# A second level of pairwise comparison in a top-k attention kernel, and another way to split its weights

## The chip, the cores and the metric

The kernel runs on one core of a Trainium2 chip. The metric is device time in microseconds (us). The engines are TensorE (PE, matmuls and transposes), VectorE (DVE), ScalarE (ACT), GpSimd (POOL) and SyncE (SP, which here issues all DMAs). Each works through its own queue in order.

## The reference

Attention with 4 batches, 8 heads, 576 positions and 64 dimensions, in which each query keeps its 32 largest scores; the result, 2304 rows of 512, goes through a gated feed-forward layer.

```python
scores = scale * np.matmul(q, k.transpose(0, 1, 3, 2))
kth = np.partition(scores, -top_k, axis=-1)[..., -top_k:-top_k + 1]
scores = np.where(scores >= kth, scores, -1000000000.0)
scores = scores - np.max(scores, axis=-1, keepdims=True)
attn = np.exp(scores)
attn = attn / (np.sum(attn, axis=-1, keepdims=True) + 1e-09)
x = np.matmul(attn, v)            # then heads side by side, 512 wide
xn = x / np.sqrt(np.mean(x * x, axis=-1, keepdims=True) + 1e-06) * rms_g
g = xn @ w_gate
out = (g / (1.0 + np.exp(-g)) * (xn @ w_val)) @ w_out
```

The three weight matrices (512 x 1536, 512 x 1536, 1536 x 512) arrive as float64.

## The kernel before

**Attends.** An attend is two heads times 128 query rows; there are 72. PE forms the scores (12 matmuls of 288 columns, fp32 split into a high and a low fp32r part), ACT copies them from PSUM into one of 5 slots `sp`, and DVE finds the 32nd largest of each row (`topk`, L492). For each of the two heads `e`, L511 and L512 take minimum and maximum of the two halves of the row: 32 values among 576 can only be among the 288 maxima and the few largest minima, so L513 appends the 8 largest minima to the maxima, and four rounds of L516 (8 largest) and L518 (replace them by a very small number) run over 296 elements. POOL turns the result into a threshold (L546) and stores a difference `gap`, from which the end of the kernel sees whether 8 minima were enough; if not, an exact second program runs (it does not here). ACT and POOL mask and exponentiate (L550 to L552), PE transposes (L575) and multiplies by V.

**Feed-forward.** When all heads of 256 query rows (a unit) are done, `feed_forward` (L627) normalizes and runs blocks: 24 matmuls for gate and value, ACT's tanh (L721), DVE's two products (L727, L728), ACT's and POOL's split into high and low part, and 6 matmuls with a slice of `w_out` in a slot `wo`. The first unit is done as two tiles of 128 rows with 6 blocks each (there a block covers two slices), eight more have 12 blocks: 108 in all.

**Weights.** In 36 pieces of 128x512 (`weight_piece`, L337), 512 KB each as float64. A piece lands in a raw tile (`xvt`, and `tg` or `kraw`, in turn), DVE joins the bits of its two words (L357 into a PSUM bank, L358 into one of three temporary tiles), ACT takes a Sign (L359) that POOL adds for rounding (L360), ACT casts the high part (L365) and POOL subtracts it for the low part (L368). The 12 slices of `w_out` also go to a scratch in DRAM (`wosc`), from which each later unit loads them again (L702) into 2 slots `wo`. All pieces are converted while the first unit is worked on.

**Order.** The program adds operations with an engine, a duration and a priority from the table `PR`; a planner (`place`, L99, with `emit`, L211) places them in a simulated time and writes each engine's queue in that order. On the chip each engine follows its queue and waits for what an instruction needs.

## Time and profile before

| | us |
|---|---|
| median of 3 runs | 877.06 (875.78 to 880.12) |
| the profiled execution | 879.04 |
| its span in the trace | 876.8 |
| busy: PE / DVE / ACT / POOL | 798.7 / 726.7 / 617.6 / 488.1 |

The span runs from the first to the last instruction of the trace. Busy time is a union: matmuls overlap, and neighbours on DVE and ACT overlap by some tens of ns, so for what an operation costs in a full queue one reads from its start to the next start, or busy time over count, rather than its mean duration.

### The profile page before, as it was taken

The numbers are of one execution on the slowest core, as the hardware profiler recorded it, in microseconds if no ns is written. First come the engines' busy times: TensorE is split into PE (matmuls) and PEld (weight loads), VectorE is DVE, ScalarE is ACT, GpSimd is POOL, SyncE is SP. The second block draws the span as 40 slices with busy tenths as digits, with TensorE's granted clock in tenths as the row PEclk, the third lists the DMA queues.
The fourth block names the chain that finished last, engine by engine and source line by source line (L and its number), as shares of the span: only waits on it lengthen the run. The fifth ranks groups of instructions, "written<-read, shape, count | busy, mean of one in ns | idle before, by whom it ended". The sixth has DMA issues, their size and how long they took to land.

```text
span 876.8 us, 19543 instructions
## 1 busy us (share of the span) xinstructions
PE 798.7 (91%) x6770; PEld 701.6 (80%) x6770; DVE 726.7 (83%) x2292; ACT 617.6 (70%) x1529; POOL 488.1 (56%) x690
## 2 busy tenths in 40 slices
PE   5656766899799999999999999999999999999996
PEld 3545745788598888989988888999889988889995
DVE  5999989999889999999899999659998469993211
ACT  6777775898687888778777887666786557874221
POOL 5778989866644564457553644665654244444121
PEclk9978766799799999999999999999999999999998
DMA  7443676455633333244343332333532252232353
GB/s 209 127 117 117 225 224 219 151 172 156 198 96 93 100 108 102 90 111 142 101 145 101 118 120 93 107 121 110 179 93 67 83 174 85 91 127 95 112 164 107
DMA packets 86653, 112.92 MB, mean 129 GB/s; under 512 B 50832, under 2 KB 64144, under 8 KB 86544
## 3 DMA queue, kind: packets, MB, share of 16 engines
q1 hardware_dynamic: 86544, 111.57, 40.8%
q8 instruction: 55, 0.90, 0.4%
q14 instruction: 54, 0.44, 0.2%
HBM read 100.53 MB, written 11.01 MB: 127 GB/s over the span
## 4 chain that ended last, share of the span: by engine, by line
PE 77%; DVE 10%; DMA 6%; ACT 3%; POOL 2%; issue 1%; SPq 0%; DVEq 0%; ACTq 0%; POOLq 0%
PE bank L321 66%; PE bank L575 8%; DVE mx L516 2%; DVE mx L518 2%; DMA wo<-wosc 2%; DMA xvt<-in_moe_w_gate_dram 2%; PE bank L425 1%; DVE bank L357 1%; PE bank L453 1%; DMA kraw<-in_k_dram 1%; DMA xvt<-in_moe_w_out_dram 1%; DVE mx L513 1%; ACT sp L552 1%; PE bank L672 1%; PE bank L637 1%
## 5 line engine op out<-in xcount | busy, mean ns | idle before, releaser
L516 DVE MAX8 mx<-mx 128x8 f32<-128x296 f32 x576 | 242.4, 455 | 0.0
L551 POOL TENSOR_TENSOR sp<-sp,rr 128x576 f32<-128x576 f32 x144 | 184.2, 1290 | 44.7 <-ACT rr L550 42.8
L518 DVE MATCH_REPLACE8 mx<-mx 128x296 f32<-128x296 f32 x432 | 192.2, 451 | 0.0
L321 PE MATMUL bank<-wo,hh 128*128 128x512 f32 x432 | 149.4, 426 | 11.8 <-DMA wo<-wosc 8.4
L740 POOL TENSOR_TENSOR hl<-tg,hh 128x256 fp32r<-128x256 f32 x108 | 79.5, 737 | 115.8 <-ACT hh L739 105.7
L575 PE MATMUL bank<-ident,sp 128*128 128x128 f32 x648 | 100.1, 286 | 29.1 <-ACT sp L552 25.5
L552 ACT ACTIVATE sp<-sp,bt 128x576 f32<-128x576 f32 x144 | 113.1, 787 | 13.7 <-POOL sp L551 13.0
L550 ACT ACTIVATE rr<-sp,bt 128x576 bf16<-128x576 f32 x144 | 108.5, 779 | 17.7 <-POOL bt L546 17.4
L539 ACT COPY sp<-bank 128x288 f32<-128x288 f32 x288 | 97.1, 409 | 24.2 <-PE bank L321 23.4
L321 PE MATMUL bank<-xth,wgh 128*128 128x256 f32 x384 | 113.5, 296 | 0.2 <-ACT xv L593 0.2
L575 PEld LDWEIGHTS bank<-ident,sp 128*128 128x128 f32 x648 | 77.6, 146 | 43.8 <-ACT sp L552 30.6
L321 PE MATMUL bank<-xth,wvh 128*128 128x256 f32 x384 | 110.5, 288 | 0.0
L321 PE MATMUL bank<-xth,wgl 128*128 128x256 f32 x384 | 107.2, 279 | 0.0
L321 PE MATMUL bank<-xtl,wgh 128*128 128x256 f32 x384 | 107.2, 279 | 0.0
L321 PE MATMUL bank<-xth,wvl 128*128 128x256 f32 x384 | 107.2, 279 | 0.0
L321 PE MATMUL bank<-xtl,wvh 128*128 128x256 f32 x384 | 107.2, 279 | 0.0
L727 DVE SCALAR_TENSOR_TENSOR tg<-tg,bank 128x256 f32<-128x256 f32 x108 | 44.3, 411 | 68.5 <-ACT tg L721 68.3
L577 ACT COPY pt<-bank 128x512 f32<-128x512 f32 x144 | 83.1, 595 | 13.1 <-PE bank L575 12.6
L321 PEld LDWEIGHTS bank<-wo,hh 128*128 128x128 f32 x432 | 71.9, 194 | 25.0 <-DMA wo<-wosc 8.3
L721 ACT ACTIVATE tg<-bank 128x256 f32<-128x256 f32 x108 | 41.3, 383 | 69.0 <-PE bank L321 55.1
L321 PE MATMUL bank<-wo,hl 128*128 128x512 f32 x216 | 86.6, 401 | 0.0
L546 POOL TENSOR_TENSOR bt<-mx,cst 128x6 f32<-128x6 f32 x72 | 14.4, 200 | 125.3 <-DVE mx L516 124.3
(147 smaller groups left out, 2052.6 us busy)
## 6 DMA issues: line engine op xcount, KB each, us to landing
wo<-wosc SPq DMA_DIRECT2D x108, 512.0 KB, 3.4
vt<-in_v_dram SPq DMA_DIRECT2D x52, 256.0 KB, 3.0
xvt<-in_moe_w_gate_dram SPq DMA_DIRECT2D x12, 512.0 KB, 4.5
wosc<-wo SPq DMA_DIRECT2D x12, 512.0 KB, 3.2
kraw<-in_k_dram SPq DMA_DIRECT2D x32, 128.0 KB, 3.1
kraw<-in_moe_w_val_dram SPq DMA_DIRECT2D x8, 512.0 KB, 4.1
qraw<-in_q_dram SPq DMA_DIRECT2D x56, 64.0 KB, 2.8
out_dram<-osb SPq DMA_DIRECT2D x14, 256.0 KB, 2.3
```

What stands on the lines that cost most here:

```text
L321: nc.tensor.matmul(o, l, r, start=start, stop=stop)
L516: add(DVE, 0.381, lambda o8=o8: nc.vector.max(o8, row[:, 0:half + 8]), w=(mk,), pri=pri + 0.1 * n)
L518: add(DVE, 0.436, lambda o8=o8: nc.vector.match_replace(row[:, 0:half + 8], o8, row[:, 0:half + 8], NEG), w=(mk,), pri=pri + 0.1 * n)
L539: add(ACT, 0.32, lambda b=bank[half, e], c0=c0: nc.scalar.copy(sp[s][:, c0:c0 + 288], b.tile[:, 0:288]), w=(("sp", s, e, half),), bank=ban ...
L550: add(ACT, 0.7, lambda e=e, tl=tl: nc.scalar.activation(rr[e], tl, AF.Relu, bias=bt[t][:, e, 2:3], scale=-BIG), r=(("bt", t),) + spkeys(i, ...
L551: add(POOL, 1.27, lambda e=e, tl=tl: nc.gpsimd.tensor_tensor(tl, tl, rr[e], op=ALU.subtract), r=(("rr", e),), w=spkeys(i, e), pri=pri + PR ...
L552: add(ACT, 0.8, lambda e=e, tl=tl: nc.scalar.activation(tl, tl, AF.Exp, bias=bt[t][:, e, 1:2], scale=SCALE, accum_out=sums(e)[0]), r=(("bt ...
L575: nc.tensor.transpose(bank.tile[:, c * 128:(c + 1) * 128], sp[s][:, c0 + c * 128:c0 + (c + 1) * 128], ident)
L577: add(ACT, 0.228 if n == 1 else 0.507, lambda dst=dst, bank=bank, n=n: nc.scalar.copy(dst[:, 0:n * 128], bank.tile[:, 0:n * 128]), w=(key, ...
L721: add(ACT, 0.325, lambda gb=gb, hs=hs: nc.scalar.activation(th[hs], gb.tile[:, 0:256], AF.Tanh, scale=1.0 if halves[0] else 0.5), w=(("th" ...
L727: add(DVE, 0.365, lambda gb=gb, hs=hs: nc.vector.scalar_tensor_tensor(th[hs], th[hs], 1.0, gb.tile[:, 0:256], op0=ALU.add, op1=ALU.mult), ...
L740: add(POOL, 0.75, lambda hs=hs: nc.gpsimd.tensor_tensor(hl[hs], th[hs], hh[hs].bitcast(F32), op=ALU.subtract), r=(("th", hs), ("hh", hs)), ...
```

## The change

- `topk` gets a second level. The 288 maxima `mw` of a row are again compared half against half: ACT copies the upper 144 of both heads into a PSUM bank (L559), DVE takes maxima (L565) and minima (L566) of 144 with that bank as one operand, and appends the 8 largest of these minima (L568). The four rounds (L573, L575) run over 160 elements. `gap` gets a second value for the new list.
- Gate weights are joined exactly by three DVE operations (L388 to L390), without Sign and POOL's addition (`HV=6`). For value and output weights the first DVE operation (L376) writes the temporary tile, not a PSUM bank, and the second (L377) reads it there.
- All 36 low parts are formed by PE: the piece times the identity, minus the high part times the negative identity `nid`, in a PSUM bank, from which ACT copies them (L399).
- Raw tiles are `xvt`, `sp[3]`, `sp[4]`, and `tg` or `kraw`, four in turn; so the first 14 attends use 3 slots `sp`, later ones 5. One temporary tile is `x[1]` in place of `x[0]`. `wo` has 3 slots.
- Other numbers of `PR` change, with an extra for the first six attends (`early`), and with them the planner's order.

```diff
-    HV=7, SU=1, ZU=6, F1=5.02, FX0=-3.08, FS0=0.39, FD0=-2.4, Z0=0, QN=0, FE=-9.01, EV=-2.13, SO=-2.7, WP1=0.21, WI=-6.69, FO=2.17, FS=0.8, ZP=0, KO=-4.26, WP0=1.0, FB=3.5, AO=0.79, FX=-16.28, QO=-3, TB=0.35, WO=-1.76, SM=1.12,
+    HV=6, SU=1, ZU=2, F1=5.43, FX0=-2.16, FS0=0.69, FD0=-4.87, Z0=0, QN=0, FE=-11.12, EV=-3.17, SO=-14.38,
...
+    GT=2, E4=14, NWT=0, MC=0.33, PL=36, AL=20,
...
-    NS, NK, NV, NQ, NPT, NWO, NQR = 5, 4, 2, 3, 4, 2, 2
+    NS, NK, NV, NQ, NPT, NWO, NQR = 5, 4, 2, 3, 4, PR["NWO"], 2
...
+            (sp[3][:, 0:1024].bitcast(U32), tuple(("sp", 3, e, half) for e in range(2) for half in range(2))),
+            (sp[4][:, 0:1024].bitcast(U32), tuple(("sp", 4, e, half) for e in range(2) for half in range(2))),
...
-                raw, rk = wraw[(0, 1 if wcnt[1] < 8 else 2)[wcnt[1] % 2]]
+                raw, rk = wraw[(0, 2, 3, 1 if wcnt[1] < 8 else 4)[wcnt[1] % 4]]
...
+                        add(DVE, 0.336, lambda: nc.vector.tensor_scalar(tu, low, 29, None, op0=ALU.logical_shift_right), r=rk, w=tk, pri=pri)
+                        add(DVE, 0.602, lambda: nc.vector.scalar_tensor_tensor(tu, top, 3, tu, op0=ALU.logical_shift_left, op1=ALU.bitwise_or), r=rk, w=tk, pri=pri, sh=True)
...
+                def left():
+                    mm(rest.tile, ident, t, True, False)
+                    mm(rest.tile, nid, hi, False, True)
+                add(PE, 1.1, left, r=tk + (keyh,), w=(keyl,), bank=rest, pri=pri)
+                add(ACT, 0.53, lambda: nc.scalar.copy(lo, rest.tile), w=(keyl,), bank=rest, pri=pri)
+                return
...
+            for op, dst, n in ((ALU.max, mw, "mw"), (ALU.min, mn, "mn")):
+                for e in range(2):
...
+                    add(DVE, 0.372, lambda e=e, b=b, op=op, dst=dst: nc.vector.tensor_tensor(dst[:, e, :], bank[e].tile[:, 0:half], b, op=op), r=bk + turn, w=((n, e),), bank=bank[e], pri=pri)
+                if n == "mw":
+                    add(ACT, 0.37, lambda: nc.scalar.copy(mc.tile[:, 0:half].rearrange("p (e c) -> p e c", e=2), mw[:, :, four:half]), r=(("mw", 0), ("mw", 1)), w=(("mc", s),), bank=mc, pri=pri + PR["MC"])
+            for e in range(2):
+                add(DVE, 0.37, lambda e=e: nc.vector.max(mx[:, e, four:four + 8], mn[:, e, :]), r=(("mn", e),), w=(("mx", e),), pri=pri)
...
+            add(DVE, 0.375, lambda: nc.vector.tensor_tensor(mx[:, :, 0:four], both(), mw[:, :, 0:four], op=ALU.max), r=wk, w=mk, bank=mc, pri=pri + 0.01)
+            add(DVE, 0.375, lambda: nc.vector.tensor_tensor(mw[:, :, four:half], both(), mw[:, :, 0:four], op=ALU.min), w=wk, bank=mc, pri=pri + 0.01)
+            for e in range(2):
+                add(DVE, 0.21, lambda e=e: nc.vector.max(mx[:, e, four + 8:four + 16], mw[:, e, four:half]), r=(("mw", e),), w=(("mx", e),), pri=pri + 0.02)
```

The first place is DVE's queue, one attend of the early stage; `mn`, `mw` and `mx` hold minima, first-level maxima and the list for the rounds. Before:

```order
L511 TENSOR_TENSOR mn<-bank_64,sp_101 128x288
L512 TENSOR_TENSOR mx<-bank_63,sp_101 128x288
L512 TENSOR_TENSOR mx<-bank_64,sp_101 128x288
L513 MAX mx<-mn 128x8 x2
L516 MAX mx<-mx 128x8 x2
L518 MATCH_REPLACE mx<-mx 128x296 x2
L516 MAX mx<-mx 128x8 x2
L518 MATCH_REPLACE mx<-mx 128x296 x2
L516 MAX mx<-mx 128x8 x2
L518 MATCH_REPLACE mx<-mx 128x296 x2
L516 MAX mx<-mx 128x8 x2
```

Now (with the first operations of the attend, and one operation of the feed-forward, L743):

```order
L557 TENSOR_TENSOR mw<-bank_64,sp_100 128x288
L557 TENSOR_TENSOR mw<-bank_68,sp_100 128x288
L557 TENSOR_TENSOR mn<-bank_64,sp_100 128x288
L557 TENSOR_TENSOR mn<-bank_68,sp_100 128x288
L561 MAX mx<-mn 128x8 x2
L565 TENSOR_TENSOR mx<-bank_65,mw 128x2x144
L566 TENSOR_TENSOR mw<-bank_65,mw 128x2x144
L568 MAX mx<-mw 128x8 x2
L743 TENSOR_TENSOR xtl<-bank_64,xth 128x4x128
L573 MAX mx<-mx 128x8 x2
L575 MATCH_REPLACE mx<-mx 128x160 x2
L573 MAX mx<-mx 128x8 x2
```

The rounds have become shorter (160 for 296), and four operations have come between the minima's maximum and the rounds, two of which read the bank that ACT fills from `mw`.

The second place is ACT's queue between the fourth and the sixth block, where most weights are converted. `wgl`, `wvl` and the second half of `wo` are low parts. Before:

```order
L359 ACTIVATE wo_76<-kraw 128x512
L539 COPY sp_98<-bank_63 128x288
L577 COPY pt_118<-bank_67 128x512
L365 CAST wo_75<-x_122 128x512
L359 ACTIVATE wgl<-xvt 128x512
L365 CAST wo_76<-osb 128x512
L359 ACTIVATE wvl<-kraw 128x512
L359 ACTIVATE wgl<-xvt 128x512
L365 CAST wgh<-qrt 128x512
L365 CAST wvh<-x_122 128x512
L359 ACTIVATE wvl<-kraw 128x512
```

Now:

```order
L391 CAST wo_77<-osb 128x512
L385 ACTIVATE wvl<-sp_102 128x512
L399 CAST wvl<-bank_65 128x512
L391 CAST wo_75<-x_125 128x512
L432 COPY pt_120<-bank_67 128x256
L612 ACTIVATE sp_99,rs_113<-sp_99,bt_111 128x576
L399 CAST wo_77<-bank_65 128x512
L399 CAST wgl<-bank_63 128x512
L399 CAST wo_75<-bank_67 128x512
L559 COPY bank_66<-mw 128x288
L610 ACTIVATE rr_104<-sp_100,bt_110 128x576
```

ACT's Sign operations (L359, now L385) have become fewer, and four copies of a low part from a bank (L399) and the operand's copy (L559) have come in among them.

The third place is SP's queue at the first reloads of `w_out` slices for the second unit. Before:

```order
L324 DMA out_dram<-osb 128x512
L324 DMA qrt<-in_q_dram 64x2x64 x2
L702 DMA wo_75<-wosc 128x1024
L702 DMA wo_76<-wosc 128x1024
L324 DMA vt_87<-in_v_dram 64x64
L324 DMA vt_87<-in_v_dram 128x2x256
L324 DMA vt_87<-in_v_dram 64x64
L702 DMA wo_75<-wosc 128x1024
L324 DMA krawt<-in_k_dram 64x2x64
L702 DMA wo_76<-wosc 128x1024
```

Now:

```order
L767 DMA wo_76<-wosc 128x1024
L338 DMA qrt<-in_q_dram 64x2x64
L767 DMA wo_77<-wosc 128x1024
L338 DMA qrt<-in_q_dram 64x2x64 x2
L338 DMA out_dram<-osb 128x512
L338 DMA vt_88<-in_v_dram 64x64
L338 DMA vt_88<-in_v_dram 128x2x256
L767 DMA wo_75<-wosc 128x1024
L767 DMA wo_76<-wosc 128x1024
L338 DMA vt_88<-in_v_dram 64x64
```

Loads into `wo` (L702, now L767) rotate over three slots, not two.

## Rows read from the trace of the kernel before

**Rows 1.** From the page: the engines' busy time with its share of the span, and the granted TensorE clock in tenths over 40 equal slices of 21.9 us.
```profile
PE 798.7 (91%) x6770; PEld 701.6 (80%) x6770; DVE 726.7 (83%) x2292; ACT 617.6 (70%) x1529; POOL 488.1 (56%) x690
...
PEclk9978766799799999999999999999999999999998
```

**Rows 2.** The windows: the span cut where blocks 4, 6 and 8 end on DVE, then at 280, 360 and 868 us. After the stretch and its length, each engine's busy us (instructions), then the granted clock, DMA share and GB/s.
```profile
core 0: us, PE busy (x) PEld busy (x) DVE busy (x) ACT busy (x) POOL busy (x), PEclk, DMA share, GB/s
0.00:112.40 112.40, 72.24 (x465) 57.33 (x466) 99.96 (x286) 83.50 (x192) 87.35 (x108) 0.86 0.54 163
112.40:153.10 40.70, 26.15 (x140) 20.37 (x139) 36.45 (x94) 26.87 (x59) 36.74 (x39) 0.64 0.65 216
153.10:174.70 21.60, 17.70 (x122) 15.37 (x122) 21.53 (x67) 17.68 (x42) 19.15 (x29) 0.76 0.46 154
174.70:280.00 105.30, 97.55 (x914) 85.00 (x913) 94.82 (x315) 84.24 (x217) 60.20 (x85) 0.95 0.47 143
280.00:360.00 80.00, 78.45 (x700) 68.88 (x700) 78.89 (x259) 64.18 (x165) 41.12 (x66) 1.00 0.33 103
360.00:868.00 508.00, 504.93 (x4431) 453.64 (x4429) 395.09 (x1277) 339.99 (x856) 243.54 (x368) 1.00 0.37 115
```

**Rows 3.** The timeline of DVE, the products that end blocks 3 and 4 (one row), 6 and 8: start us, us, line, operation, out<-in.
```profile
111.64 0.75 DVE L728 TENSOR_TENSOR tg<-tg,bank 128x256 f32<-128x256 f32 x2
...
152.64 0.42 DVE L728 TENSOR_TENSOR tg<-tg,bank 128x256 f32<-128x256 f32 x1
...
174.28 0.42 DVE L728 TENSOR_TENSOR tg<-tg,bank 128x256 f32<-128x256 f32 x1
```

**Rows 4.** The timeline of DVE within one attend and two weight operations; what counts is from one start to the next.
```profile
65.18 0.45 DVE L512 TENSOR_TENSOR mx<-bank,sp 128x288 f32<-128x288 f32 x1
65.54 0.81 DVE L513 MAX8 mx<-mn 128x8 f32<-128x288 f32 x2
66.27 0.82 DVE L516 MAX8 mx<-mx 128x8 f32<-128x296 f32 x2
67.00 0.07 DVE L518 MATCH_VALUE_LOAD mx<-mx 128x8 f32 x1
67.06 0.45 DVE L518 MATCH_REPLACE8 mx<-mx 128x296 f32<-128x296 f32 x1
67.43 0.08 DVE L518 MATCH_VALUE_LOAD mx<-mx 128x8 f32 x1
...
71.83 0.68 DVE L357 TENSOR_SCALAR bank<-kraw 128x512 uint32<-128x512 uint32 x1
72.41 0.69 DVE L357 TENSOR_SCALAR bank<-xvt 128x512 uint32<-128x512 uint32 x1
73.00 0.45 DVE L511 TENSOR_TENSOR mn<-bank,sp 128x288 f32<-128x288 f32 x1
```

**Rows 5.** DVE's groups by form: count | busy us, mean ns of one | idle before.
```profile
L658 DVE TENSOR_SCALAR rw<-ss 128x2 int32<-128x2 int32 x8 | 7.2, 902 | 0.1
...
L358 DVE SCALAR_TENSOR_TENSOR osb<-xvt,bank 128x512 uint32<-128x512 uint32 x6 | 4.1, 688 | 0.4
...
L657 DVE TENSOR_SCALAR ss<-ss 128x2 f32<-128x2 f32 x8 | 4.1, 509 | 3.1 <-ACT bank L651 3.1
...
L555 DVE TENSOR_SCALAR rs<-rs 128x8 f32<-128x8 f32 x16 | 2.6, 161 | 6.2 <-ACT sp L552 6.2
...
L658 DVE TENSOR_SCALAR rw<-ss 128x1 int32<-128x1 int32 x2 | 0.3, 141 | 0.0
```

**Rows 6.** The timeline of POOL and DVE at one start of L657.
```profile
317.20 1.29 POOL L652 TENSOR_TENSOR x<-x,gt 128x512 f32<-128x512 f32 x1 [0.35 <-ACT bank L651]
...
317.33 1.18 DVE L657 TENSOR_SCALAR ss<-ss 128x2 f32<-128x2 f32 x1
```

**Rows 7.** The waits of DVE from 0 to 180 us: us in total, times, longest.
```profile
DVE bank L357 <- DMA xvt<-in_moe_w_gate_dram: 1.9, 3, 1.1
...
DVE mn L511 <- ACT sp L539: 1.4, 2, 1.2
...
DVE mx L512 <- POOL bt L546: 0.6, 1, 0.6
```

**Rows 8.** ACT's groups by form, as in rows 5.
```profile
L552 ACT ACTIVATE sp<-sp,bt 128x576 f32<-128x576 f32 x144 | 113.1, 787 | 13.7 <-POOL sp L551 13.0
L550 ACT ACTIVATE rr<-sp,bt 128x576 bf16<-128x576 f32 x144 | 108.5, 779 | 17.7 <-POOL bt L546 17.4
L539 ACT COPY sp<-bank 128x288 f32<-128x288 f32 x288 | 97.1, 409 | 24.2 <-PE bank L321 23.4
L577 ACT COPY pt<-bank 128x512 f32<-128x512 f32 x144 | 83.1, 595 | 13.1 <-PE bank L575 12.6
...
L552 ACT ACTIVATION_READ_ACCUMULATOR sp<-sp,bt 128x1 f32 x144 | 28.7, 200 | 0.0
...
L359 ACT ACTIVATE wgl<-xvt 128x512 fp32r<-128x512 f32 x12 | 8.2, 681 | 4.3 <-DMA xvt<-in_moe_w_gate_dram 4.2
```

**Rows 9.** The timeline of PE at full clock: eight transposes of 128 columns, and two groups of three 512-column fp32r matmuls.
```profile
339.74 1.04 PE L575 MATMUL bank<-ident,sp 128*128 128x128 f32 x8
340.54 0.37 PE L321 MATMUL bank<-xth,wgh 128*128 128x256 f32 x1
...
344.52 0.73 PE L321 MATMUL bank<-wo,hh 128*128 128x512 f32 x2
...
345.33 0.63 PE L321 MATMUL bank<-wo,hh 128*128 128x512 f32 x2
```

**Rows 10.** The waits of PE from 174.7 us to the end.
```profile
PE bank L321 <- DMA wo<-wosc: 8.4, 5, 3.5
```

More of the change, by code (lines that the diff above doesn't have):

```diff
@@ L39, with early @@
 SWITCH = 0.2
+def early(name, i):
+    return PR[name] + (PR[name + "E"] if i < PR["E0"] else 0)
 class _Bank:
@@ L296, in tile_topk_attention_moe @@
     ident = sb("ident", [128, 128])
+    nid = sb("nid", [128, 128], F32R)
     one = sb("one", [128, 1])
-    cst = sb("cst", [128, 2, 3])
+    kb = sb("kb", [128, 1])
+    cst = sb("cst", [128, 2, 4])
     gt = sb("gt", [128, DM])
+    wt = [sb(f"wt{i}", [128, DM]) for i in range(PR["NWT"])]
     ss = sb("ss", [128, 2])
@@ L483, in prep_q_tail, with place_of @@
             return turned(lambda z: qrt[:, 2 * half + z].rearrange("p h d -> p (h d)"), (("qrt", half, 0), ("qrt", half, 1)), pri)
-        rounds = (slice(310, 318), slice(296, 304), slice(296, 304), slice(318, 326))
+        rounds = (slice(167, 175), slice(176, 184), slice(176, 184), slice(168, 176))
+        def place_of(i):
+            return i % 3 if i < PR["E4"] and not exact else i % NS
         def spkeys(i, *es):
-            return tuple(("sp", i % NS, e, half) for e in es for half in range(2))
@@ L492, in topk, with topk_exact @@
-        def topk(i, e, bank, pri):
-            s, spk = i % NS, spkeys(i, e)
-            mk, nk = ("mx", e, 0), ("mn", e, 0)
-            half = S // 2
-            row = mx[:, e, :]
-            if exact:
-                work = mx.rearrange("p e c -> p (e c)")[:, 0:S]
-                t8 = mn.rearrange("p e c -> p (e c)")
-                keys = (("mx", 0, 0), ("mx", 1, 0))
+            return tuple(("sp", place_of(i), e, half) for e in es for half in range(2))
+        def topk_exact(i, e, pri):
+            s, spk = place_of(i), spkeys(i, e)
+            work = mn.rearrange("p e c -> p (e c)")
+            t8 = mx.rearrange("p e c -> p (e c)")
+            keys, tk = (("mn", 0), ("mn", 1)), (("mx", e),)
+            for n in range(4):
+                src, sk = (sp[s][:, e * S:(e + 1) * S], spk) if n == 0 else (work, keys)
+                o8 = t8[:, 64 * e + 8 * n:64 * e + 8 * n + 8]
+                add(DVE, 0.67, lambda o8=o8, src=src: nc.vector.max(o8, src), r=sk, w=tk, pri=pri)
+                if n < 3:
+                    add(DVE, 0.67, lambda o8=o8, src=src: nc.vector.match_replace(work, o8, src, NEG), r=tk + sk, w=keys, pri=pri)
@@ L503, in topk @@
                 for n in range(4):
-                    src, sk = (sp[s][:, e * S:(e + 1) * S], spk) if n == 0 else (work, keys)
-                    o8 = t8[:, 64 * e + 8 * n:64 * e + 8 * n + 8]
-                    add(DVE, 0.67, lambda o8=o8, src=src: nc.vector.max(o8, src), r=sk, w=(nk,), pri=pri)
+                    o8, top = row[:, rounds[n]], row[:, 0:four + 16]
+                    add(DVE, 0.237, lambda o8=o8, top=top: nc.vector.max(o8, top), w=mk, pri=te + 0.1 * n)
                     if n < 3:
-                        add(DVE, 0.67, lambda o8=o8, src=src: nc.vector.match_replace(work, o8, src, NEG), r=(nk,) + sk, w=keys, pri=pri)
@@ L514, in topk @@
-            for n in range(4):
-                o8 = row[:, rounds[n]]
-                add(DVE, 0.381, lambda o8=o8: nc.vector.max(o8, row[:, 0:half + 8]), w=(mk,), pri=pri + 0.1 * n)
-                if n < 3:
-                    add(DVE, 0.436, lambda o8=o8: nc.vector.match_replace(row[:, 0:half + 8], o8, row[:, 0:half + 8], NEG), w=(mk,), pri=pri + 0.1 * n)
+                        add(DVE, 0.294, lambda o8=o8, top=top: nc.vector.match_replace(top, o8, top, NEG), w=mk, pri=te + 0.1 * n)
         def attend(i, cols, qs, sums, pri):
-            s, t = i % NS, i % 2
+            s, t = place_of(i), i % 2
@@ L538, in attend @@
                     c0 = e * S + half * 288
-                    add(ACT, 0.32, lambda b=bank[half, e], c0=c0: nc.scalar.copy(sp[s][:, c0:c0 + 288], b.tile[:, 0:288]), w=(("sp", s, e, half),), bank=bank[half, e], pri=pri + PR["SO"])
-            for e in range(2):
-                topk(i, e, bank[0, e], pri + PR["TB"] * e)
+                    add(ACT, 0.32, lambda b=bank[half, e], c0=c0: nc.scalar.copy(sp[s][:, c0:c0 + 288], b.tile[:, 0:288]), w=(("sp", s, e, half),), bank=bank[half, e], pri=pri + early("SO", i))
@@ L554, in invert @@
+                add(POOL, 1.27, lambda e=e, tl=tl: nc.gpsimd.tensor_tensor(tl, tl, rr[e], op=ALU.subtract), r=(("rr", e),), w=spkeys(i, e), pri=pri + early("SM", i))
+                add(ACT, 0.8, lambda e=e, tl=tl: nc.scalar.activation(tl, tl, AF.Exp, bias=bt[t][:, e, 2:3], scale=SCALE, accum_out=sums(e)[0]), r=(("bt", t),), w=spkeys(i, e) + (sums(e)[1],), pri=pri + early("SM", i))
         def invert(rslot, sl, keys, key, pri):
```

118 lines of the change are left out of this document (74 added, 44 removed).

## Prediction

> **What bounds the kernel now.** The first view read is the page's busy shares [rows 1]: TensorE (PE) 91%, VectorE (DVE) 83%, none above. These are averages over two different stages, so the windows come next [rows 2]. From 280 to 868 us PE is busy for 583.4 of 588 us at the full clock: PE sets the time there, and DVE, ACT and POOL have room. Before that PE is starved: from 0 to 174.7 us it is idle for 174.7 - 72.2 - 26.2 - 17.7 = 58.6 us, and its granted clock is 0.86, 0.64 and 0.76, a mix of its levels 1.2 and 2.4 GHz. I cut this early time where DVE ends the fourth, sixth and eighth feed-forward block (L728 at 111.64, the second of a pair, 152.64 and 174.28) [rows 3], because a block's second matmul waits for that product. Up to block 4 DVE is busy 100.0 of 112.4 us; between blocks 4 and 6 POOL (36.7) and DVE (36.5) share 40.7 us; between 6 and 8 DVE alone fills 21.5 of 21.6 [rows 2]. So the length of the early stage is set by DVE, helped by POOL in the middle, and what PE does after block 8 is nearly fixed.
>
> The change can only win by making block 8 earlier, or by removing PE's idle and half-clock time behind it. In the two orders PE has nearly the same matmuls left behind its eighth block: 62 of 80 score groups (a tail attend counts twice) and 97.5 or 98 of 108 block products, so I take that rest as equal.
>
> **DVE, by counts of the order times durations.** Start to start, a 288-wide operation takes 0.37 us (65.18 to 65.54, and two in 0.73), a 296-wide maximum 0.365, a match-and-replace with its value load 0.43 (67.00 to 67.43), and a 512-wide operation 0.59 (71.83 to 72.41) [rows 4]. From 288 to 512 elements that is 0.98 ns each, so at 160 elements the maximum is 0.365 - 136 x 0.00098 = 0.232, the replacement 0.297, and the 144-wide maximum 0.225. One attend was 6 x 0.37 + 8 x 0.365 + 6 x 0.43 = 7.7 us. Now it is 4 first-level operations, 2 maxima of 288 and 2 second-level operations (8 x 0.37), 2 x 0.225, 8 x 0.232 and 6 x 0.297 = 7.05. That is 0.65 us for each of 72 attends; but behind block 8 PE covers it, so only the attends ahead of block 8 count, and the new order has 15 of them there, not 13.
>
> Weights: 36 pieces at 0.59 + 0.66 (L358: 4.1 / 6 with a stall for its operand) [rows 4, 5] = 1.25. Now 12 gate pieces take three operations, 0.59 + 2 x 0.66 = 1.91, and 24 pieces the pair L376/L377. L376 reads and writes SBUF, which no 512-wide row does. Its ends are 0.59 (the same size with PSUM output [rows 4]) and 0.16 (the 8-element L555, SBUF to SBUF [rows 5]); I take 0.40, nearer to the row of its own size. With L377 at 0.66 the pair is 1.06. The Trainium skill, "VectorE: DVE Perf Modes", section on the perf-mode tiers, gives an fp32 scalar operation within SBUF twice the rate; by its 58 + FD/2 cycles an estimate for L376 is 0.33, and the sum would be 1.7 us lower. No row here shows it.
>
> Ahead of block 4: before, 54 operations of 0.37, 68 maxima, 51 replacements, 21 pieces = 93 us; now 80 of 0.37, 19 x 0.225, 72 x 0.232, 54 x 0.297, 9 gate pieces and 14 pairs = 98.7. The difference of 5.7 on 100.0 busy gives 105.7. Between 4 and 6, 34.9; between 6 and 8, 25.0 (three attends where two were).
>
> **DVE against POOL.** L376 and L377 work within SBUF while POOL may be running. L555 does that at 0.161 us, as short as it can be; L657 and L658 take 0.509 and 0.902 on average in the two-column form, which starts just behind a POOL multiply of 1.29 us and lasts until it ends (317.33 + 1.18 against 317.20 + 1.29), and 0.141 in the one-column form [rows 5, 6]. The loss per operation lies between 0 and 0.76. I take 0.1, nearest to L555, because only L657 and L658 are released by the same event as the POOL operation that they meet: 2.8, 1.8 and 0.2 us in the three stretches.
>
> **DVE's other idle time** before block 4, 12.4 us, stays, but for the waits of L512 for POOL (0.6: the first write is now to `mw`, not `mx`) and of L357 for raw tiles (1.9: four tiles rotate, not two) [rows 7]. What is late next there is the K load of the second pairs, behind one more 512 KB piece on SP's queue; I count it as hidden by the weight pieces that DVE then has, and as 2 us if not.
>
> **POOL and ACT.** POOL loses 36 subtractions and 12 additions, all early, and stops being a bound. ACT gains 36 copies of the low part and 72 of the operand, and loses 12 Sign operations. Between blocks 4 and 6 its order has 11 low-part copies (0.577 like L577), 2 operand copies (0.337 like L539), 2 more Relu (0.753), 4 more Exp (0.785 + 0.2) and some 5 narrow copies (2.0), and 2 Sign, 2 casts and 4 L539 fewer (3.9) [rows 8]: 26.9 + 10.6 = 37.5 us, against DVE's 34.9 + 1.8. So ACT takes POOL's place and the stretch is 38, not 40.7. ACT's wait for its new operand copy is costed at nothing: DVE has 2 x 0.37 + 2 x 0.37 = 1.48 us of other work between the operand and its use, the copy takes 0.34 and ACT may be 1.1 us late. Without that cover one Exp pair more in front costs 0.9 us per attend: behind the waiting L565 on DVE's queue stand the rounds, for which POOL's threshold, ACT's Relu and PE's transposes of that attend wait.
>
> **PE's extra work.** Each of 36 pieces adds a 512-column fp32 product (as eight 128-column transposes in 0.8 us: 0.43 [rows 9]) and a 512-column fp32r one (three in 0.81: 0.27), 0.7 us, or 1.4 at half clock: 25 to 50 us, beside 58.6 us of PE idle. A product might cost more than transposes of its width; twice would be 15 us more, and still fit. Hidden; if half of it fell on PE's path it would cost 12 us. Six banks serve it, since L376 no longer takes one. Three score slots (not five) for the first 14 attends are hidden by 2 x 7 us of DVE work.
>
> **Behind block 8.** Before: 702.1 us. PE waited 8.4 us there for reloads of `wo` [rows 10]; the third slot lets each load start one block earlier, some 5 us, longer than any of the waits (3.5 at most). The clock of 0.95 over 97.6 us busy [rows 2] is 4.9 us lost, of which I return 4. So 702.1 - 8.4 - 4 = 689.7.
>
> **Sum.** 105.7 + 12.4 - 2.5 + 2.8 = 118.4; + 38 + 25.2 = 181.6 at block 8, 7 us later than before, with two attends more behind it; + 689.7 = 871.3 us, 5.5 below the span of 876.8. The profiled execution took 879.04, 2.24 more than its span; the median is 877.06. With 5.5 off, 871.5. About 0.5% is what this kernel's measurement can tell from nothing: 872.7 to 881.4 counts as the same.
>
> **Rivals.**
> *Clean start* (0.30): L376 near 0.3 and no meetings with POOL (118.4 - 4 = 114.4, then 35.9 and 24.7: block 8 at 175), and none of the 4 us of PE idle that I left behind it: 689.7 - 4 = 685.7, together 861. For: POOL goes from 143 us busy up to block 8 [rows 2] to some 87, so it is seldom in DVE's way. Against: ACT then has to follow at 90%.
> *ACT is the new bound* (0.14): the operand copy waits behind an Exp pair in every second of the 15 attends: 15 x 0.9 / 2 = 6.7, so 878, no change. For: up to block 8 ACT has 128.1 us busy [rows 2] + 36 x 0.577 + 15 x 0.337 - 12 x 0.68 + 12 for the two attends more = 158 of 182, 87%, in one queue in order. Against: DVE waited for ACT's score copies for only 1.4 us there [rows 7].
> *The port* (0.14): L376 and L377 lose what L658 loses, 0.76 each, on 48 operations on DVE's path: 36.5 us instead of 4.8, 903; at half of it 887. It decides from 4.8 + 10 = 14.8 / 48 = 0.31 us per operation on, above which the kernel is slower than before. The rows of L657 and L658 speak for it, L555 against. The Trainium skill, "GPSIMD Engine Reference", Specifications, says that GpSimd shares its SBUF interfaces with VectorE, contending with VectorE instructions in a two-port mode or with two SBUF inputs; L376 would be the first kind, L377 the second. L658's row agrees for the first kind; none here shows the second.
> My forecast, 863 to 878 around 871.5, has 0.42. That `wo` still waits is inside it.
>
> **Chances.** Faster by over 0.5%: 0.27 of the forecast's 0.42 (its lower side), all of the clean start, 0.02 of ACT = 0.59. Same: 0.14 of the forecast, 0.08 of ACT, 0.02 of the port = 0.24. Slower: 0.01, 0.04 and 0.12 of these three = 0.17. The range that leaves out a tenth on each side goes from the clean start with some luck, 853, to the port at half price, 888.
>
> **What would show it.** Right: the eighth product of the early stage at 176 to 186 us, L573 near 0.23 and L575 with its load near 0.30 start to start, L376 and L377 at most 0.1 us above their shortest, ACT above 85% before block 8, no wait for `wo` above 1 us, and PE fully busy from block 8 on. Wrong: L377 of 1 us and more beside POOL's operations; DVE waiting for the copy in `mc`; PE idle still after 190 us; or PE's own products of the low part on the chain of waits.

## The result and the profile after

The changed kernel takes 856.25 us (855.83 to 856.53, 4 runs), the kernel before 878.3 beside it; the ratio is 0.975, 95% interval 0.9722 to 0.9779. The forecast was 871.5: the direction was right, but 5.5 us were promised and 22 came. The time lies below the 863 to 878 of the forecast itself and nearest to the 861 of the clean start. That is luck, since the clean start's conditions (block 8 at 175 us, no meetings of DVE with POOL) did not come true, as shown below. The profiled span is 854.2 us, not 876.8. From the page, engines and granted clock [rows 1]:

```profile
PE 806.6 (94%) x6878; PEld 692.3 (81%) x6878; DVE 679.1 (80%) x2592; ACT 642.1 (75%) x1626; POOL 437.9 (51%) x643
PE   5777898999899999999999999999999999999996
PEclk9998999999999999999999999999999999999998
```

The slices with a low clock are gone and PE's early slices are fuller. The windows, cut where blocks 4, 6 and 8 end on DVE, columns as in [rows 2]:

```profile
0.00:116.50 116.50, 85.94 (x537) 58.08 (x537) 105.35 (x356) 95.17 (x225) 60.12 (x85) 0.96 0.56 173
116.50:155.40 38.90, 34.52 (x212) 22.88 (x210) 36.69 (x117) 35.55 (x81) 22.88 (x25) 1.00 0.68 225
155.40:183.00 27.60, 27.16 (x235) 22.23 (x236) 25.79 (x99) 25.87 (x69) 18.44 (x31) 1.00 0.58 186
183.00:280.00 97.00, 93.72 (x882) 81.36 (x881) 89.45 (x371) 83.90 (x223) 59.55 (x85) 1.00 0.47 141
280.00:360.00 80.00, 80.00 (x743) 71.17 (x744) 75.10 (x310) 68.19 (x180) 41.17 (x64) 1.00 0.33 101
360.00:854.00 494.00, 485.28 (x4277) 436.55 (x4275) 346.73 (x1347) 333.43 (x853) 235.80 (x356) 1.00 0.37 116
```

DVE's products that end those blocks, from its timeline [rows 3]:

```profile
116.13 0.40 DVE L795 TENSOR_TENSOR tg<-tg,bank 128x256 f32<-128x256 f32 x1
155.01 0.42 DVE L795 TENSOR_TENSOR tg<-tg,bank 128x256 f32<-128x256 f32 x1
182.61 0.40 DVE L795 TENSOR_TENSOR tg<-tg,bank 128x256 f32<-128x256 f32 x1
```

They end at 116.5, 155.4 and 183.0 us, against the forecast's 118.4, 156.4 and 181.6: by DVE's mark the early stage came out nearly as summed. So the error lies behind it: 854.2 - 183.0 = 671.2 us, where I had 689.7. The missing 18.5 us have two parts.

**What PE had done by then.** PE's groups up to DVE's eighth product, first of the kernel before (0 to 174.7 us), then of the changed one (0 to 183); the number behind x is what counts:

```profile
L575 PE MATMUL bank<-ident,sp 128*128 128x128 f32 x95 | 21.0, 356 | 26.6 <-ACT sp L552 24.5 <-ACT pt L577 0.9 <-ACT tg L737 0.6
L321 PE MATMUL bank<-kh,qh 64*128 64x288 f32 x56 | 16.2, 476 | 14.9 <-DVE qrt L358 6.2 <-ACT bank L651 4.0 <-ACT tg L737 1.2
L321 PE MATMUL bank<-pt,vt 128*64 128x128 f32 x144 | 15.2, 359 | 0.0
L321 PE MATMUL bank<-wo,hh 128*128 128x512 f32 x20 | 9.6, 541 | 3.4 <-POOL wo L368 3.4
L321 PE MATMUL bank<-ptt,vt 128*64 128x128 f32 x36 | 5.5, 398 | 1.9 <-ACT pt L577 1.0 <-ACT ptt L577 0.9
```

```profile
L635 PE MATMUL bank<-ident,sp 128*128 128x128 f32 x126 | 20.4, 297 | 12.2 <-ACT sp L612 6.3 <-DVE mw L566 2.5 <-ACT wo L399 2.0
L335 PE MATMUL bank<-pt,vt 128*64 128x128 f32 x208 | 15.2, 286 | 0.9 <-ACT pt L637 0.9
L335 PE MATMUL bank<-kh,qh 64*128 64x288 f32 x60 | 13.8, 371 | 2.6 <-DVE qrt L390 0.8 <-DVE x L390 0.7 <-DVE mw L566 0.6
L335 PE MATMUL bank<-wo,hh 128*128 128x512 f32 x24 | 8.5, 427 | 0.3 <-ACT wo L399 0.3
L335 PE MATMUL bank<-ptt,vt 128*64 128x128 f32 x52 | 6.2, 321 | 1.0 <-ACT ptt L637 0.7 <-DVE qrt L390 0.2
```

31 score transposes, 64 + 16 products with V, 12 score products (4 of each of three kinds), a block's 6 output products, 13 gate and value products and 6 small transposes more are done. Each is priced from start to start. A transpose takes 0.10 us and an output product 0.27 [rows 9], a gate or value product 0.117 (below), and from PE's timeline in the changed kernel 4 and 16 products with V take 0.27 and 0.97 us, and 12 score products 1.0 us (121.88 to 122.88):

```profile
119.35 0.44 PE L335 MATMUL bank<-ptt,vt 128*64 128x128 f32 x4
119.62 1.04 PE L335 MATMUL bank<-pt,vt 128*64 128x128 f32 x16
120.59 1.12 PE L335 MATMUL bank<-qrt,ident 128*128 128x512 f32 x2
...
121.88 0.40 PE L335 MATMUL bank<-kh,qh 64*128 64x288 f32 x2
...
122.88 1.12 PE L335 MATMUL bank<-x,ident 128*128 128x512 f32 x2
```

That is 3.1 + 3.9 + 1.1 + 1.0 + 1.6 + 1.5 + 0.6 = 12.8 us. (Busy time over count, from the groups behind block 8, would give 18.6 us and seem to explain everything. But in PE's queue different groups overlap: there they sum to 1219 us, where PE is busy for 659.)

**What the same matmuls took.** A gate or value product of 256 columns, at the granted clock of 1.00 in both kernels, first and last of 18 in a row, before and now:

```profile
509.07 0.28 PE L321 MATMUL bank<-xth,wgh 128*128 128x256 f32 x1
...
511.06 0.28 PE L321 MATMUL bank<-xth,wvl 128*128 128x256 f32 x1
```

```profile
502.48 0.28 PE L335 MATMUL bank<-xth,wgh 128*128 128x256 f32 x1
...
504.42 0.28 PE L335 MATMUL bank<-xth,wvl 128*128 128x256 f32 x1
```

17 steps take 1.99 us before and 1.94 now. Over some 1900 such steps behind 280 us in each trace the median is 117 ns before and 114 now. For the 2304 products of this kind behind block 8 that is 7 us, which no term of the forecast had.

Together: PE is busy 682.6 us behind DVE's mark before and 659.0 now, 23.6 less. Some 12.8 of it is work that is done already, 4.9 the clock, and the remaining 6 the shorter matmuls. PE's idle time there fell from 19.5 to 12.2 us, by 7.3. The forecast had 4 for the clock and 8.4 for the idle time: the 18.5 us are 12.8 + 6 and these small differences.

**Where PE was.** PE's first output product of block 8, in the kernel before and in the changed one:

```profile
200.37 0.50 PE L321 MATMUL bank<-wo,hh 128*128 128x512 f32 x1
```

```profile
196.01 0.48 PE L335 MATMUL bank<-wo,hh 128*128 128x512 f32 x1
```

And the windows from DVE's eighth product to it, in the same order:

```profile
174.30:200.40 26.10, 26.10 (x266) 22.74 (x265) 23.91 (x80) 23.07 (x62) 15.19 (x19) 1.00 0.60 179
```

```profile
182.60:196.00 13.40, 13.40 (x138) 11.89 (x137) 11.07 (x45) 10.60 (x29) 6.09 (x10) 1.00 0.38 125
```

PE is busy all of that time at full clock. It did not wait for the product: it had 26 us of older work in front of it before the change, 13 after. By PE's own mark block 8 came 4.4 us earlier; by DVE's, 8.3 us later. Behind PE's mark the rest is 676.4 us before and 658.2 now. There the forecast's own subtraction gives 676.4 - 8.4 - 4 = 664.0, and only 5.8 us are left over, as much as the shorter matmuls.

### The profile page after: what moved, and what is told of

The parts are those of the page before. It is cut to its first block, busy times and chain, and to the rows that moved or that the text cites. A ratio compares the mean times of both kernels' runs of the same rounds, so it can differ in the third digit from the quotient of the medians.

```text
span 854.2 us, 20177 instructions
## 1 busy us (share of the span) xinstructions
PE 806.6 (94%) x6878; PEld 692.3 (81%) x6878; DVE 679.1 (80%) x2592; ACT 642.1 (75%) x1626; POOL 437.9 (51%) x643
## 4 chain that ended last, share of the span: by engine, by line
PE 73%; DVE 13%; ACT 5%; DMA 4%; POOL 2%; issue 1%; SPq 1%; DVEq 0%; POOLq 0%; ACTq 0%
PE bank L335 63%; PE bank L635 7%; DVE mx L573 2%; DVE mx L575 2%; DMA kraw<-in_k_dram 1%; DMA sp<-in_moe_w_out_dram 1%; DVE mx L561 1%; PE bank L488 1%; DVE mw L557 1%; PE bank L460 1%; PE bank L698 1%; ACT rr L610 1%; ACT sp L596 1%; ACT sp L612 1%; SPq L338 1%
## 5 line engine op out<-in xcount | busy, mean ns | idle before, releaser
L573 DVE MAX8 mx<-mx 128x8 f32<-128x160 f32 x576 | 158.2, 311 | 0.0
L335 PE MATMUL bank<-wo,hh 128*128 128x512 f32 x432 | 144.0, 414 | 1.2 <-DMA wo<-wosc 0.9
L575 DVE MATCH_REPLACE8 mx<-mx 128x160 f32<-128x160 f32 x432 | 130.1, 307 | 0.0
L335 PE MATMUL bank<-xth,wgh 128*128 128x256 f32 x384 | 111.4, 290 | 0.7 <-DVE mw L566 0.4
L635 PE MATMUL bank<-ident,sp 128*128 128x128 f32 x648 | 96.7, 279 | 13.0 <-ACT sp L612 6.3
L635 PEld LDWEIGHTS bank<-ident,sp 128*128 128x128 f32 x648 | 75.8, 143 | 27.8 <-ACT sp L612 8.6
L557 DVE TENSOR_TENSOR mw<-bank,sp 128x288 f32<-128x288 f32 x144 | 61.3, 447 | 44.9 <-ACT sp L596 44.7
```

The costliest lines, as they stand in the source:

```text
L335: nc.tensor.matmul(o, l, r, start=start, stop=stop)
L557: add(DVE, 0.372, lambda e=e, b=b, op=op, dst=dst: nc.vector.tensor_tensor(dst[:, e, :], bank[e].tile[:, 0:half], b, op=op), r=bk + turn, ...
L573: add(DVE, 0.237, lambda o8=o8, top=top: nc.vector.max(o8, top), w=mk, pri=te + 0.1 * n)
L575: add(DVE, 0.294, lambda o8=o8, top=top: nc.vector.match_replace(top, o8, top, NEG), w=mk, pri=te + 0.1 * n)
L635: nc.tensor.transpose(bank.tile[:, c * 128:(c + 1) * 128], sp[s][:, c0 + c * 128:c0 + (c + 1) * 128], ident)
```

## The experiments

Two kinds of run have to be kept apart. A part that is undone or done alone is planned anew, and every engine's order changes with it. In the runs called "same order" one kind of instruction is doubled, shrunk or added, and the other engines' instructions stay in their places. "Block 8" is the end of DVE's eighth product, as above. Long lines of the edits are broken up here, and ... stands for lines left out.

### Parts of the change, planned anew

**Low parts by GpSimd again** (changed kernel).

```diff
-    GT=2, E4=14, NWT=0, MC=0.33, PL=36, AL=20,
+    GT=2, E4=14, NWT=0, MC=0.33, PL=0, AL=20,
```

> The changed kernel, with the low parts of all 36 weight pieces taken on GpSimd again (36 subtractions of some 1.3 us), and without the two products of TensorE and the copy of ScalarE. Three theories for the 18 us that the time behind block 8 was shorter than I worked out. Backlog: with less work on GpSimd the softmax of an attend ends sooner after its thresholds, so that TensorE has done more transposes and products when VectorE ends block 8. Then 866 to 874 us here, TensorE idle for ScalarE's exponentials for 20 us and more, and some 95 to 105 score transposes done at block 8 instead of 126. Clock: the products of the low part keep TensorE's granted clock at 0.96 and more in the early stage, and that alone brings the rest forward. Then also 864 to 872, but with a granted clock of 0.65 to 0.85 over 40 to 160 us. Thresholds: only VectorE's shorter attends matter. Then 852 to 858 here, as block 8 would come at 180 to 186 us again.

875.65 us, ratio to before 0.997 (0.9947 to 0.9994): nearly all is lost. PE waits 28.3 us for exponentials, and the clock is 0.57 to 0.79 in the three stretches of 40 us from 40 to 160 us. But DVE's block 8 is late as well (199.8 us, with 131 score transposes done), which no theory had, so backlog and clock are not told apart here. That only the shorter attends matter (852 to 858) has fallen.

**Two products on PE that nothing reads, subtraction still on GpSimd** (kernel before).

```diff
+            add(PE, 1.1, left, r=tk + (keyh,), bank=rest, pri=pri)
             add(
                 POOL, 1.24,
```

> The kernel before, with the two products of each weight piece on TensorE as in the changed kernel, into a bank that nothing reads; the low part itself stays with GpSimd. This gives TensorE the activity without the relief of GpSimd. Clock: the early granted clock rises from 0.64 to 0.86 to 0.9 and more, and the time falls to 860 to 868. Backlog: GpSimd is as loaded as before, TensorE waits for the exponentials as before, so 874 to 882 whatever the clock. Thresholds: 874 to 882 as well.

886.07 us, 1.009 (1.0063 to 1.0117), although the clock rises to 0.97 in 80 to 120 us. The clock that the added products keep up doesn't pay for them here.

**One level of pairs** (changed kernel; the old 296-wide rounds, no operand copy).

> The changed kernel, with the thresholds found as before the change: one level of pairs, 296-wide maxima and replacements, no operand copy by ScalarE. VectorE has 0.65 us more per attend, so some 10 us more ahead of block 8. Thresholds: most of the gain is gone, 868 to 876 us. Backlog: block 8 comes later by up to 10 us, but the softmax and TensorE follow as closely as now, so 860 to 866. Clock: with the granted clock still at 0.95 and more, 858 to 864.

876.02 us, 0.9975 (0.9958 to 0.9993). Nearly all is lost again, which is the upper end of what the shorter attends alone would have given (868 to 876). But DVE's block 8 is only 3 us later (186.3), not 10, while the transposes of the 20th attend come at 265 us, not 243. And the gate and value products take 117 ns again.

**Two slots for the reloaded weights** (changed kernel, `NWO=2`).

> The changed kernel with two slots for the reloaded output weights, not three. In the kernel before, TensorE waited 8.4 us for these reloads behind block 8; I gave the third slot all of it. If so, 862 to 866 us here and waits of some 8 us. If the waits were only the other side of a TensorE that was late for other reasons, 854 to 858.

863.69 us, 0.9832 (0.979 to 0.9873). The time is what the waits would give, but the waits are not there. From the waits of PE in this run, behind block 8:

```profile
PE bank L335 <- DMA wo<-wosc: 1.7, 2, 1.1
```

DVE's block 8 comes at 188.8 us: the loss has moved to the early stage of a new order.

**Low parts by PE alone** (kernel before).

```diff
+            add(PE, 1.1, left, r=tk + (keyh,), w=(keyl,), bank=rest, pri=pri)
+            add(ACT, 0.53, lambda: nc.scalar.copy(lo, rest.tile), w=(keyl,), bank=rest, pri=pri)
+            return
             add(
                 POOL, 1.24,
```

> The kernel before, with the low parts of the weight pieces by TensorE and ScalarE as the only change. If this part alone carries the gain (relief of GpSimd, or the clock): 858 to 866. If VectorE's one-level thresholds then set the early stage, as in the run with one level: 872 to 882.

891.76 us, 1.0154 (1.012 to 1.0189): slower than either theory had.

**Second level alone, and both** (kernel before, its own table of numbers).

> The kernel before, by its own table, with the second level of pairs and ScalarE's operand copy alone; low parts by GpSimd. With the low parts by TensorE alone it took 891.8, with both 868.1. If the parts add up, the second level alone would be worth 23.7 us: 853 to 858. If they need each other, since GpSimd's queue holds the early stage until both are there: 872 to 882.

> The kernel before, by its own table, with two parts of the change alone: the second level of pairs with ScalarE's operand copy, and the low parts by TensorE and ScalarE. Two raw tiles, two slots for the reloaded weights, the gate pieces' old path. If these two parts carry the gain once they come together: 860 to 868. If the raw tiles, the third slot and the new table are as large a part: 870 to 882.

866.52 (0.985, 0.9807 to 0.9894) and 868.06 us (0.9878, 0.985 to 0.9907). The second level alone is worth 12 us, with DVE's block 8 at 164.5 us, and gate and value products of 114 ns. The low parts on PE lose 13 alone; beside the second level the loss of 1.5 is within the noise. They don't add up, but the first doesn't need the second either: both expectations of the first run fell, and the second run lies at the upper edge of its first range.

**Two raw tiles** (changed kernel, two entries of `wraw`, `E4=0`).

> The changed kernel with two raw tiles for the weights, not four, and five score slots from the start. I gave the raw tiles 1.9 us of VectorE's waits. If that was all: 854 to 859. If the pieces' chain (load, VectorE, ScalarE, TensorE, ScalarE) holds a raw tile long enough to stall VectorE: 862 to 872, with waits of VectorE for raw tiles of over 5 us before block 8.

865.4 us, 0.9842 (0.9821 to 0.9862): 9 us are lost, as the second theory had, and with the waits that it named, though the fifth score slot from the start (`E4=0`) is changed in this run too. Up to block 8 DVE waits 8.4 us for raw tiles. In the changed kernel the same waits are 9.6 us, but 7.6 of these are the time before DVE's first instruction, which there is a weight operation; here those first 7.7 us are put down to ACT's copy of K (L454). So 8.4 us stand against 2.0, and block 8 comes 7 us later (190.0).

**The old table of numbers** (changed kernel, all parts kept).

> The changed kernel with every part of the change, but the planner's numbers that the kernel before had too are set back to its values and the six early ones are off. The prediction gave the new numbers nothing of their own. If so: 854 to 859. If the order that they make (which attends stand ahead of which block) carries a part: 862 to 872.

858.6 us, 0.9776 (0.9734 to 0.9817): 2.3 us more than the changed kernel, within the noise, as forecast.

**A third slot alone** (kernel before).

> The kernel before with a third slot for the reloaded output weights, nothing else. The prediction gave it all of the 8.4 us of TensorE's waits: 868 to 872. In the changed kernel two slots cost 7.4 us, though with waits of 1.7 us only. If the waits hide another lateness: 874 to 882.

885.87 us, 1.0073 (1.0047 to 1.0099). The waits for `wo` are gone, and others have come or grown. From the waits of PE in the whole run:

```profile
PE bank L575 <- POOL sp L601: 7.4, 1, 7.4
PE bank L321 <- POOL wo L368: 5.0, 3, 2.5
```

One more buffer, which lets loads start earlier and lengthens no operation, costs 7 us through the order. So a single run that is planned anew can't price a part to better than that.

### Same order

**Tiny products** (changed kernel; the low parts of the weights are zero).

```diff
-                    mm(rest.tile, ident, t, True, False)
-                    mm(rest.tile, nid, hi, False, True)
+                    mm(rest.tile[:, 0:8], ident, t[:, 0:8], True, True)
...
-                add(ACT, 0.53, lambda: nc.scalar.copy(lo, rest.tile), w=(keyl,), bank=rest, pri=pri)
+                add(ACT, 0.53, lambda: nc.scalar.mul(lo, rest.tile[:, 0:1].to_broadcast([128, 512]), 0.0),
+                    w=(keyl,), bank=rest, pri=pri)
```

> The changed kernel in the same order on every engine, but the two 512-column products of each weight piece are one of 8 columns, and ScalarE writes the low parts as zeros (so the low parts of the weights are missing from the output). GpSimd is relieved as in the changed kernel; TensorE has some 42 us less to do in the early stage. Clock: without these products the granted clock falls back to 0.65 to 0.85 over 40 to 160 us, TensorE is late again, and the time is 860 to 870. Backlog: the exponentials come as early as now, TensorE follows VectorE as closely, and the time is 848 to 857, whatever the clock shows. If the products lie on the path (not hidden at all), 825 to 840.

858.45 us, 0.9769 (0.9748 to 0.9789), which is the changed kernel's time within the noise. Without the products PE is no earlier. The windows from 0 to 280 us, of the kernel before, the changed one and this one:

```profile
0.00:280.00 280.00, 213.64 (x1637) 178.07 (x1638) 252.76 (x758) 212.28 (x508) 203.44 (x259) 0.85 0.53 162
```

```profile
0.00:280.00 280.00, 241.34 (x1861) 184.55 (x1862) 257.28 (x938) 240.48 (x596) 160.99 (x223) 0.98 0.55 170
```

```profile
0.00:280.00 280.00, 223.71 (x1805) 189.07 (x1806) 258.08 (x925) 238.68 (x591) 158.21 (x222) 0.90 0.55 169
```

Of all PE instructions (6770, 6878 and 6842, with the products) 5133, 5017 and 5037 are left behind 280 us. By kind, and at the mean from start to start, the 116 fewer of the changed kernel are worth some 12 us, and the 96 fewer here 10. Behind 280 us PE is idle for 11.7, 8.9 and 8.9 us. The remaining 8 of the 22.6 us are matmuls that take less time at the same clock, in this run as in the changed kernel. So about half of the gain is PE's advance, and it comes without the products: they take idle and half-clock time (the clock is 0.98 with them and 0.90 without) at no cost.

**Double products** (changed kernel).

```diff
+                    for _ in range(2): mm(rest.tile, ident, t, True, False), mm(rest.tile, nid, hi, False, True)
```

> The changed kernel in the same order on every engine, with both products of each weight piece done twice: some 42 us more of TensorE work in the early stage, where TensorE has 35 us idle up to block 8. Hidden work: 854 to 862, with the idle time filled. Half on the path: 870 to 880. All on the path: 890 to 900.

871.57 us, 0.9912 (0.9889 to 0.9936). PE is 34.4 us busier (841.0), or 0.96 for each of 36 pairs. Some 15 of the 34 are on the path. So the first pair of products just fits, a second doesn't.

**GpSimd as loaded as before** (changed kernel; `junk` is read by nothing).

```diff
                 nc.gpsimd.tensor_tensor(tl, tl, rr[e], op=ALU.subtract)
+                if i < 18:
+                    four = ident.unsqueeze(1).to_broadcast([128, 4, 128])
+                    nc.gpsimd.tensor_tensor(junk, four, four, op=ALU.subtract)
```

> The changed kernel in the same order on the other engines; on GpSimd each of the first 36 softmax subtractions is followed by one more subtraction of 512 columns that nothing uses, some 1.25 us each, 45 us in all, as much as the 36 subtractions of the low part were. TensorE's products stay. Backlog: GpSimd is again as loaded as before the change, the exponentials and so TensorE's transposes come later, 866 to 876 us, with waits of TensorE for exponentials of 15 us and more. If the loss in the first run came from the weight pieces' own chain (GpSimd's subtraction late in it) and not from GpSimd's load: 855 to 860.

865.51 us, 0.9857 (0.9823 to 0.9891). A load of 41 us on GpSimd costs 9 us in this order; it stands in other places of GpSimd's queue than the subtractions of the low part did. PE's waits for exponentials are 6.7 us, as without the load (6.3), so the loss doesn't come by way of them as expected. DVE's block 8 comes at 192.9 us. Up to it DVE is busy 171.9 us with the same 568 instructions that took 167.8, so part of the loss is DVE's own operations beside POOL's.

**More work for DVE, behind block 8, and ahead of it with `i < 15`** (changed kernel).

```diff
                 nc.vector.max(mx[:, e, four:four + 8], mn[:, e, :])
+                if 15 <= i < 27:
+                    nc.vector.max(junk, mn[:, e, :])
```

> The changed kernel in the same order; VectorE does the 288-wide maximum of attends 15 to 26 twice, 24 operations of 0.37 us, 8.9 us more, all behind block 8. My prediction's step: TensorE covers VectorE there, so 854 to 858. Rival: VectorE still sets the pace up to about block 20, so that a shorter attend counts there too: 860 to 866.

> The changed kernel in the same order; VectorE does the 288-wide maximum of the first 15 attends twice, 30 operations of 0.37 us, 11.1 us more, all ahead of block 8. My prediction's step: VectorE sets this stage, block 8 comes 9 to 11 us later and the time is 864 to 868. Rival: TensorE has enough behind VectorE there (it is idle for 35 us only) that half of it is hidden: 858 to 863.

861.31 (0.9797, 0.9765 to 0.9829) and 862.92 us (0.982, 0.979 to 0.985): 5.1 of 8.9 us and 6.7 of 11.1 come through, about half in both places, each to within some 4 us. So behind block 8 PE doesn't fully cover DVE in the changed kernel, and ahead of it DVE doesn't set the time alone.

**The same behind block 8 in the kernel before** (`13 <= i < 25`).

> The kernel before in its own order; VectorE does the 288-wide maximum of attends 13 to 24 twice, 24 operations of 0.37 us, 8.9 us more, all behind its block 8. The prediction took TensorE as the bound from there on: 877 to 881, as the kernel before. If VectorE sets the pace up to about block 20 here too: 883 to 888.

879.81 us, 1.0014 (0.9994 to 1.0033): nothing that can be measured. Here PE did cover DVE.

**GpSimd relieved in the kernel before** (the low parts of the weights are zero).

```diff
-                lambda: nc.gpsimd.tensor_tensor(lo, t, hi.bitcast(F32), op=ALU.subtract),
+                lambda: nc.gpsimd.memset(lo.bitcast(F32), 0.0),
```

> The kernel before in its own order on every engine; GpSimd's 36 subtractions of the low part (1.24 us) are fills with zero (so the low parts of the weights are missing from the output). Backlog: with GpSimd free, the exponentials that TensorE waits for (24.5 us) and the weights come earlier and TensorE reaches its eighth block well before 200 us: 862 to 870. If GpSimd's load was not what made TensorE late, but its order and its clock: 874 to 879.

877.34 us, 0.9993 (0.9977 to 1.0009): nothing. A fill takes 0.53 us, so GpSimd is 27 us less busy (460.9), not 45, and PE waits for exponentials nearly as before (24.5):

```profile
PE bank L575 <- ACT sp L552: 23.8, 13, 4.2
```

The backlog theory has fallen as far as these 27 us go: in the old order GpSimd's load is not what makes PE late.

**Products in PE's waits in the kernel before.**

```diff
                 def tr(bank=bank, c0=c0, n=n):
+                    if i < 14:
+                        mm(bank.tile, ident, ident.unsqueeze(1).to_broadcast([128, 4, 128]), True, True)
                     for c in range(n):
```

> The kernel before in its own order on every engine; ahead of the transposes of each of the first 14 attends TensorE does three more products of 512 columns, in the banks that the transposes then write: 42 of some 0.64 us, 27 us, that need no operand but the identity and so can run while it waits for the exponentials. Clock: the granted clock of 40 to 175 us rises from 0.64 to 0.86 to 0.9 and more, and TensorE reaches block 8 earlier: 864 to 872. If the clock cost little, because TensorE mostly waits there: 876 to 884. All on the path: 900 and more.

892.19 us, 1.0153 (1.0122 to 1.0183). The clock is 0.92 (0.86 before) up to 112 us and 0.71 (0.64) up to 153, and still 14 us are lost. PE is 31 us busier (829.8), so the clock gave back less than the products cost: the clock theory, by which they would have won 6 to 14 us, has fallen too. What a higher clock without added work would be worth, this run can't say.

## Why the forecast was half right

**Right.** The sum of the early stage: 183.0 against 181.6 at block 8. By stretches it is off by -1.9, +0.9 and +2.4 us, so errors cancel in part. DVE is busy 105.35 of 116.5 us up to block 4 (105.7 + 2.8 were summed). The parts, from DVE's timeline, start to start:

```profile
68.92 0.53 DVE L573 MAX8 mx<-mx 128x8 f32<-128x160 f32 x2
69.37 0.07 DVE L575 MATCH_VALUE_LOAD mx<-mx 128x8 f32 x1
69.43 0.30 DVE L575 MATCH_REPLACE8 mx<-mx 128x160 f32<-128x160 f32 x1
69.66 0.07 DVE L575 MATCH_VALUE_LOAD mx<-mx 128x8 f32 x1
...
129.88 0.41 DVE L376 TENSOR_SCALAR osb<-sp 128x512 uint32<-128x512 uint32 x1
130.20 0.45 DVE L565 TENSOR_TENSOR mx<-bank,mw 128x288 f32<-128x288 f32 x1
```

The maximum takes 0.45 / 2 = 0.225 (0.232), the replacement with its load 0.29 (0.297), an undisturbed L376 0.32 (0.40). ACT is busy 156.6 of 183 us, 86% (87%), and DVE waits for the copy in `mc` 3.0 us in the whole run: ACT did not become the bound. The waits for `wo` fell from 8.4 to 0.9 us, and from 183 us on the clock is 1.00, as the 4 us returned had it.

**The port** stayed small. L376's 24 operations are busy 15.6 us, 0.65 each against the shortest 0.40; L377's 17.6 us, 0.73 against 0.67. That is 7.4 us for the two, where I took 4.8, and 36.5 was the rival. The sign "at most 0.1 us above their shortest" failed for L376, which is 0.25 above. The Trainium skill, "GPSIMD Engine Reference", Specifications, names both kinds as contending with GpSimd. The trace agrees for L376 (1.35 us at 65.89, where a POOL operation started at 65.68), while L377, with two SBUF inputs, mostly shows nothing, but for a few at 1.04. By the Trainium skill, "VectorE: DVE Perf Modes", the estimate for L376 alone was 0.33; the 0.32 agrees.

**Mis-sized without effect.** A pair of PE's products takes 1.2 us on the timeline (122.88 to 124.08), not 0.7: 43 us, not 25 (35 by the double-products run's 0.96). I had said that 15 us more would still fit, and they did; the tiny-products run shows the products hidden.

**The step that failed.** "In the two orders PE has nearly the same matmuls left behind its eighth block ..., so I take that rest as equal", and the reason for the cut, "because a block's second matmul waits for that product". The equality holds at PE's own eighth block: 18 of the 80 score groups are done there in both kernels. But the sum was cut at DVE's product, at which PE wasn't waiting: PE came to it 26 us later, busy throughout, and in the new order 13 us later. So 702.1 - 8.4 - 4 = 689.7 carried some 12.8 us of work over into the new kernel's rest that was done there already. The note "with two attends more behind it" had the cause in it and got no price: by then PE has transposed 14 attends' scores (126 / 9), not 10.6 (95 / 9). The other 6 us are in "equal" itself: the same matmuls were taken to cost the same, and they took less. Measured: 671.2.

That DVE's mark is no measure shows in other runs too. It comes at 164.5 us with the second level alone (866.5 us), at 168.8 with the third slot alone (885.9) and at 175.5 with the old table of numbers (858.6), against 174.7 before and 183.0 in the changed kernel. Within one order it does say something: double products, GpSimd's load and DVE's early work put it back by 17, 10 and 8 us, and the time by 15, 9 and 7.

**Not confirmed.** The 8.4 us of the third slot: the waits went, but each run that moved the slot alone paid or gained in another place. The 1.9 us for raw tiles were too few: with two tiles DVE waits 8.4 us for them up to block 8, with four 2.0 behind its first instruction, and the time differs by 9 us (in a run planned anew).

**What stays open.** Two things are shown: PE's advance, 12 us by 280 us, and matmuls that are 8 us shorter behind it. Neither has a shown cause.

In the old order neither 27 us less for GpSimd nor added products shorten the time; in the new order the advance is there. In that order the loads are tight together: DVE's added work counts about half, GpSimd's 9 of 41 us, the products nothing until doubled. Which part of the change lets the planner find that order can't be told: the losses from undoing one part each (19, 20, 7, 9 and 2 us) sum to over twice the gain. A rival is untried: that DVE's shorter attends ahead of block 8 would bring a part in the old order too. There only longer ones behind block 8 were run.

The shorter products go with the second level: the median is 117 ns in all eight kernels with one level and 114 in all twelve with two, whatever their order. While DVE is idle it is nearly the same (117 before, 113 now). The second level also changes the sizes of DVE's tiles, which may move other tiles in SBUF; whether that is the cause no run tests.

## What to carry to other kernels

Cut a span where the engine that sets the end stands, and count in the trace what it has done at that moment. Another engine's milestone is no measure of it when the first has older work queued. Price that work from start to start: where groups overlap, busy time over count is too much, and here it made half an explanation look like a whole one. Then look whether the same instructions still take the same time. Where a planner sets the order, price a part in an unchanged order (double or shrink its instructions), since one buffer more, planned anew, moved the time by 7 us. A relief that other engines' slack can swallow has to be tried in the order that it will run in: 27 us off GpSimd were worth nothing in one order, and 41 us on it cost 9 in the other.
